# Splitting weights in one ScalarE pass, mixing in two matmul passes, and a later place for two steps of the next batch

## The chip, the cores and the metric

The kernel runs on one core of a Trainium2 chip. The metric is the device time of one execution in microseconds (us). A core has five engines that run their own instruction streams in order and wait for each other by semaphores: TensorE (PE: matmuls, and PEld, its weight loads), VectorE (DVE), ScalarE (ACT), GpSimd (POOL) and SyncE (SP), which here issues transfers between HBM and the on-chip memory SBUF. Matmuls write to PSUM banks. Times inside a run are us from the start of the span, the time from the first to the last instruction.

## The reference

Three blocks follow each other, for 8 batches of 576 rows (`S`), 8 heads of 64, 32 memory slots and a model width of 512:

```
a    = softmax(phi)                       # over the 576 rows
k_m, v_m = a^T k, a^T v                   # 32 slots per head
x    = softmax(q k_m^T / 8) v_m           # attention output, [576, 512]
h    = x^T U V                            # mixing over the rows, rank 32
u    = x + h^T
y    = u + relu(u w_ch1) w_ch2            # 512 -> 2048 -> 512
hh   = relu(y w_in);  u, v = halves of hh # 512 each
v_s  = w_spatial normalize(v) + b         # mixing over the rows
out  = (u * v_s) w_out
```

The matrices arrive in 32 bits (several of them as float64 values, which the kernel turns into 32-bit ones itself).

## The kernel before, in words

The work runs batch by batch, in half batches of 288 columns (`TH`), with five row tiles of 128 (`NST`; the fifth, the rest tile, has 64 rows). From batch 1 on, a factor is kept as two 16-bit halves, an upper and a lower one, and a product is three matmuls that add up in PSUM: upper by upper, upper by lower, lower by upper. Where the code says `for x, y in HI`, these are the three index pairs. An f32 matmul, used in batch 0, leaves two records in the profile.

Weights are loaded once. In batch 0 they are used in 32 bits while `conv_stream` converts them, and then `split_chunk` turns a chunk of 512 columns (288 for `w_spatial`) into the halves, in the place of the 32-bit chunk: ScalarE scales the chunk into a temporary tile (line 135), ScalarE copies it to the upper half (line 139), and VectorE subtracts to get the lower half (line 140). There are 54 chunks: `si` are those of `w_in` (8), `sw` of `w_spatial` (10), `s1` and `s2` of the two big matrices (16 each), `so` of `w_out` (4).

These splits, the norms of the spatial weights (`sn`), the conversion (`cs`) and the attention of batch 1 (`a1`) are generators. A `Filler` (lines 1020 to 1056) takes turns among those that are handed to it, a step at a time, as long as a budget lasts, and so mixes them into the matmul loops; `finish` runs one to its end. A scheduler then settles the order on each engine. Every engine's stream is fixed before the kernel runs.

The attention `att` of the next batch is spread in the same way over the loops of the present batch. Its parts here: the sums over rows of the softmax times U, the product `pps` (line 622, three matmuls per row tile, 96 columns of weights); `apr_sum` (lines 498 to 512), which adds the product with V and the attention weights themselves, transposed by a matmul with a scaled identity (line 509), in the three `at` banks; the largest value, spread over the partitions by a matmul with ones of a diagonal tile (`bmax_a` makes the diagonal, `bmax_b` issues the matmul, line 124); and the scaling into halves `apr` (lines 662 and 663), which empties the `at` banks. Behind it `z_gen` computes z, a product with w1 (line 693), again into `at` banks, 8 yields apart.

The stages of a batch are w1 (line 768; 722 in batch 0), w2 (line 805; 745 in batch 0), the scaling of y (`y_finish`), v and u (lines 876 and 945), spatial mixing with the gate (line 982), and the output (line 1005). In batch 0 the filler of the v and u stage has `a1, s1, so, s2`, and that of the spatial stage `a1, so, s1, s2`.

Of the kernel before, what the change touches and what calls it, by code (L numbers as in the profile page):

```python
# [30 lines left out]
def mixer_kernel(  # L31
# [52 lines left out]
    u3h = cp.tile([128, 2, NST, 96], F16, name="u3h")  # L84
    vst = cp.tile([96, S], F16, name="vst")
# [66 lines left out]
    def load_static():  # L152
        act.dma_start(ident, consts[:, 0:128])
        dve.memset(onesb, 1.0)
        pool.memset(ones32, 1.0)
        pool.memset(kmt, 0.0)

# [109 lines left out]
    def first(vr):  # L267
# [135 lines left out]
        ahl = tp.tile([128, NST, 2, 256], F16, tag="pa", name="ahl")  # L403

# [13 lines left out]
        def mix(ss):  # L418
            if not pps:
                pps.append(at_tile())  # L420
            for s in ss:
                r = rows(s)
                for i, (x, y) in enumerate(HI):
                    pe.matmul(pps[0][0:96, 0:256], u3h[:r, x, s, :], ahl[:r, s, y, :],
                              start=(s == 0 and i == 0), stop=(s == NST - 1 and i == 2))
# [19 lines left out]
        uh, ul = (u3h[:, i].rearrange("p s (e c) -> p s e c", c=M) for i in range(2))  # L445
        pool.tensor_copy(uh, ub)
        pool.tensor_tensor(out=ul, in0=ub, in1=uh, op=ALU.subtract)
# [5 lines left out]
        for h in range(2):  # L453
            act.activation(vst[:, h * TH:(h + 1) * TH], vr[1 + h][0], func=ACTF.Copy)
# [5 lines left out]
        for h in range(2):  # L460
            sl = slice(h * TH, (h + 1) * TH)
            pool.tensor_tensor(out=vst[32:64, sl], in0=vr[1 + h][0][32:64], in1=vst[32:64, sl], op=ALU.subtract)
        conv_b(*z0)
# [17 lines left out]
        pst = tp.tile([96, 256], F16, tag="pst", name="pst")  # L481
        act.activation(pst, pps[0][0:96, 0:256], func=ACTF.Copy, scale=2.0 ** -22)
# [15 lines left out]
    def apr_sum(pst, ahl, parts):  # L498
        ps = at_tile()
        o = 0  # L500
        for g, sa, sb in parts:
            n = min(sb * 128, S) - sa * 128
            pe.matmul(ps[:, o:o + n], pst[0:96, g * 128:(g + 1) * 128], vst[0:96, sa * 128:sa * 128 + n],
                      start=True, stop=False)
            for s in range(sa, sb):
                r = rows(s)
                for l in range(2):
                    oo = o + (s - sa) * 128
                    pe.matmul(ps[:, oo:oo + r], ahl[:r, s, l, g * 128:(g + 1) * 128], ident16[:r, :r],
# [4 lines left out]
    def att(b):  # L514
# [67 lines left out]
        ahl = tp.tile([128, NST, 2, 256], F16, tag="pa", name="ahl")  # L582
        for grp in ((0, 1), (2, 3), (4,)):
# [35 lines left out]
        for s in range(NST):  # L619
            r = rows(s)  # L620
# [802 lines left out]
```

## Time and profile before

| | us |
|---|---|
| median of 3 runs | 1189.0 (1183.98, 1189.0, 1189.25) |
| profiled execution | 1188.7 |
| its span | 1186.8 |
| TensorE busy in it | 1156.0 |
| VectorE busy | 690.3 |
| ScalarE busy | 533.5 |
| GpSimd busy | 65.4 |
| mean granted TensorE clock | 0.993 of 2.4 GHz |

Busy times are unions of an engine's instructions, so overlaps count once. A matmul's duration of 287 ns is the time through the array; the next one starts earlier, so that the pace of a stream is read from the start of one group to the start of the next. A bracket behind a row of the order of time is the idle time of that engine just before, with the instruction that ended it.

### The profile page before, as it was taken

What the parts mean: (1) busy time and instruction counts of PE and PEld (TensorE: products, weight loads), DVE (VectorE), ACT (ScalarE), POOL (GpSimd) and SP (SyncE); (2) the same over time, 40 slices, a digit from 0 to 9 for tenths busy, and PEclk for the clock granted to TensorE, in tenths of its full rate; (3) what the DMA queues carried; (4) which work ended last, traced back from release to release, by engine and by line L of the source; (5) the groups of instructions that cost most, each with busy time, mean ns of one, the idle gap of its engine ahead of it and who ended that gap; (6) DMA issues with size and microseconds to landing.
All of it is one profiled execution on the core that took longest, in us unless ns stands there. A gap on an engine that the chain in (4) does not pass through costs nothing.

```text
span 1186.8 us, 24260 instructions
## 1 busy us (share of the span) xinstructions
PE 1156.0 (97%) x10036; PEld 860.9 (73%) x10039; DVE 690.3 (58%) x1893; ACT 533.5 (45%) x1219; POOL 65.4 (6%) x251
## 2 busy tenths in 40 slices
PE   8898999899999999999999999999999999999998
PEld 6566767577677776777767776777767787677767
DVE  5766578657475474635665464754646465652454
ACT  4768885556245143442434242451434433442333
POOL 2001010000000000000000000100000000000000
PEclk9999999899999999999999999999999999999999
DMA  9776200140001400032001300014000200010001
GB/s 345 318 262 216 77 21 2 61 124 19 21 1 44 139 21 1 22 101 61 22 1 41 119 24 21 1 41 141 22 1 16 71 23 1 1 41 1 2 1 40
DMA packets 43005, 73.80 MB, mean 62 GB/s; under 512 B 6608, under 2 KB 34000, under 8 KB 39824
## 3 DMA queue, kind: packets, MB, share of 16 engines
q1 hardware_dynamic: 42384, 71.59, 17.8%
q8 instruction: 78, 1.28, 0.5%
q10 hardware_dynamic: 512, 0.67, 0.2%
q14 instruction: 31, 0.25, 0.1%
HBM read 62.82 MB, written 9.44 MB: 61 GB/s over the span
## 4 chain that ended last, share of the span: by engine, by line
PE 83%; DVE 6%; ACT 4%; DMA 4%; issue 1%; POOL 1%; POOLq 0%; ACTq 0%
PE mm L805 25%; PE mm L768 14%; PE mm L1005 8%; PE mm L945 7%; PE mm L982 7%; PE mm L876 6%; PE mm L745 4%; DMA kvt<-in_kv_dram 3%; PE at L590 2%; PE at L693 1%; PE at L540 1%; DMA qt<-in_qT_dram 1%; PE at L622 1%; PE mm L722 1%; PE mm L873 1%
## 5 line engine op out<-in xcount | busy, mean ns | idle before, releaser
L805 PE MATMUL mm<-g,w2r 128*128 128x288 f16 x2688 | 349.1, 287 | 0.0
L805 PEld LDWEIGHTS <-w2r 128*128 128x128 f16 x2688 | 257.6, 98 | 76.9 <-issue 14.2
L768 PE MATMUL mm<-apr,z 128*128 128x288 f16 x1344 | 167.5, 286 | 0.0
L768 PEld LDWEIGHTS <-z 128*128 128x128 f16 x1344 | 131.2, 98 | 32.9
L823 ACT ACTIVATE y<-mm 128x288 f32<-128x288 f32 x56 | 22.7, 406 | 208.0 <-DVE tiny L130 208.0
L777 DVE TENSOR_TENSOR g<-tmp,g 128x288 f16<-128x288 f32 x224 | 99.2, 456 | 20.1 <-ACT g L774 16.9
L982 PE MATMUL mm<-wsr,vu 128*128 128x288 f16 x768 | 104.7, 286 | 0.0
L772 ACT ACTIVATE tmp<-mm 128x288 f32<-128x288 f32 x224 | 91.7, 421 | 28.7 <-PE mm L768 14.5
L130 DVE TENSOR_REDUCE tiny<-mm 128x1 f32<-128x288 f32 x64 | 28.8, 453 | 124.1 <-PE mm L805 123.4
L1005 PE MATMUL mm<-ghl,wor 128*128 128x288 f16 x768 | 98.8, 290 | 0.0
L945 PE MATMUL mm<-yhl,wir 128*128 128x288 f16 x768 | 96.8, 286 | 0.0
L1005 PEld LDWEIGHTS <-wor 128*128 128x128 f16 x768 | 75.7, 99 | 26.4 <-issue 6.0
L945 PEld LDWEIGHTS <-wir 128*128 128x128 f16 x768 | 74.5, 98 | 21.6 <-issue 1.6
L982 PEld LDWEIGHTS <-vu 128*128 128x128 f16 x768 | 74.5, 98 | 18.7 <-DVE vu L928 0.3
L876 PE MATMUL mm<-wir,yhl 128*128 128x512 f16 x384 | 86.3, 379 | 0.0
L992 ACT ACTIVATE ghl<-vu,ysc 128x288 f16<-128x288 f32 x64 | 34.2, 534 | 83.3 <-DVE vu L991 61.6
L876 PEld LDWEIGHTS <-yhl 128*128 128x128 f16 x384 | 37.1, 98 | 41.4 <-issue 0.2
L745 PE MATMUL mm<-g,w2r 128*128 128x288 f32 x256 | 65.6, 408 | 0.1
L745 PEld LDWEIGHTS mm<-g,w2r 128*128 128x128 f32 x256 | 47.7, 190 | 15.2 <-issue 2.5
L776 DVE CAST g<-tmp 128x288 f16<-128x288 f32 x112 | 34.3, 306 | 41.0 <-ACT tmp L772 40.4
L1009 ACT ACTIVATE tmp<-mm,ysc 128x288 f32<-128x288 f32 x64 | 31.7, 497 | 38.6 <-PE mm L1005 37.6
L774 ACT ACTIVATE g<-mm 128x288 f16<-128x288 f32 x112 | 46.7, 417 | 0.0
(276 smaller groups left out, 1476.5 us busy)
## 6 DMA issues: line engine op xcount, KB each, us to landing
kvt<-in_kv_dram SPq DMA_DIRECT2D x28, 516.0 KB, 4.4
out_dram<-tmp SPq DMA_DIRECT2D x64, 144.0 KB, 1.7
qt<-in_qT_dram SPq DMA_DIRECT2D x28, 256.0 KB, 3.3
wir<-in_w_dram SPq DMA_DIRECT2D x6, 1024.0 KB, 7.7
e<-in_phi_dram SPq DMA_DIRECT2D x8, 512.0 KB, 4.1
phiT<-in_phiT_dram SPq DMA_DIRECT2D x7, 576.0 KB, 3.6
wor<-in_w_dram SPq DMA_DIRECT2D x3, 1024.0 KB, 7.0
wsr<-in_w_dram SPq DMA_DIRECT2D x3, 1024.0 KB, 6.8
```

Of the source, the lines that this page charges most:

```text
L745: pe.matmul(ps, w2r[:, f, d * 128:(d + 1) * 128], AT[0]["g"][:, f, :], start=False, stop=(f == 15))
L768: pe.matmul(ps, a["z"][:, k, x, f * 128:(f + 1) * 128], a["apr"][:, k, y, sl], start=(i == 0), stop=(i == 5))
L772: act.activation(r, ps, func=ACTF.Relu, scale=CG)
L774: act.activation(g[:, f, 0, :], ps, func=ACTF.Relu, scale=CG)
L776: dve.tensor_copy(g[:, f, 0, :], r)
L777: dve.tensor_tensor(out=g[:, f, 1, :], in0=r, in1=g[:, f, 0, :], op=ALU.subtract)
L805: pe.matmul(pss[d], w2h[:, f, x, d * 128:(d + 1) * 128], g[:, f, y, :], start=False, stop=(f == 15 and i == 2))
L876: pe.matmul(ps, yhl[:, k, x, s * 128:(s + 1) * 128], wih[:, k, 1, y, :], start=(i == 0), stop=(i == 11))
L945: pe.matmul(ps, wih[:, k, 0, x, d * 128:(d + 1) * 128], a["yhl"][:, k, y, sl], start=(i == 0), stop=(i == 11))
L982: pe.matmul(ps, vn[:, s, x, ds], wsh[:, s, th, y, :], start=(i == 0), stop=False)
L992: act.activation(ghl[:, d, 0, sl], u2, func=ACTF.Identity, scale=sgt)
L1005: pe.matmul(ps, woh[:, k, x, d * 128:(d + 1) * 128], a["ghl"][:, k, y, sl], start=(i == 0), stop=(i == 11))
```

## The change

- The halves of a weight change places: the lower comes first in memory. A chunk is now split by one ScalarE pass, which writes the scaled chunk in 16 bits to a temporary tile; VectorE computes the lower half from the 32-bit chunk in its place (a scalar_tensor_tensor), and then copies the upper half behind it. Every matmul that reads these weights takes the other index.
- The mixing product takes two matmuls per row tile. The weights have 128 columns: three copies of U's upper half, and its lower half; the second matmul has the three copies and a block of zeros. V gets a fourth block of 32 rows. The rest tile's lower 64 rows of `ahl` are set to zero by GpSimd, and all its matmuls have 128 rows.
- `third`, the filler of the second w1 half of batch 0, gets the splits of `w_in` from its fifth call on and the norms from its ninth, where it had the splits from the first and the norms from the fourth.
- The filler of the v and u stage of batch 0 has `a1, so`; `so` is finished before the spatial stage, whose filler has `a1, s1, s2`.
- `att_z` yields four times instead of twice before `z_gen`.

```diff
-    def split_chunk(raw, hi, lo, s, on_dve):
-        n = raw.shape[-1]
-        r = tmp()[:raw.shape[0], :n]
+    def split_chunk(raw, lo, hi, s):
+        r = tmp().bitcast(F16)[:, 0:raw.shape[-1]]
         act.activation(r, raw, func=ACTF.Identity, scale=s)
-        if on_dve:
-            dve.tensor_copy(hi, r)
-        else:
-            act.activation(hi, r, func=ACTF.Copy)
-        dve.tensor_tensor(out=lo, in0=r, in1=hi, op=ALU.subtract)
+        dve.scalar_tensor_tensor(out=lo, in0=raw, scalar=s, in1=r, op0=ALU.mult, op1=ALU.subtract)
+        dve.tensor_copy(hi, r)
...
         ahl = tp.tile([128, NST, 2, 256], F16, tag="pa", name="ahl")
+        pool.memset(ahl[64:128, 4], 0.0)
...
         for s in range(NST):
-            r = rows(s)
-            for i, (x, y) in enumerate(HI):
-                pe.matmul(pps[0:96, 0:256], u3h[:r, x, s, :], ahl[:r, s, y, :],
-                          start=(s == 0 and i == 0), stop=(s == NST - 1 and i == 2))
+            for y in range(2):
+                pe.matmul(pps[:, 0:256], u3h[:, y, s, :], ahl[:, s, y, :],
+                          start=(s == 0 and y == 0), stop=(s == NST - 1 and y == 1))
...
-        yield
-        yield
+        for _ in range(4):
+            yield
         yield from z_gen(b)
...
-            fl(1.5, cs, a1, si, *(() if nf[0] < 4 else (sn,)))
+            fl(1.5, cs, a1, *(() if nf[0] < 5 else (si,)), *(() if nf[0] < 9 else (sn,)))
...
-        vfill = (lambda dt: fl(dt, a1, s1, so, s2)) if b == 0 else (lambda dt: None)
+        vfill = (lambda dt: fl(dt, a1, so)) if b == 0 else (lambda dt: None)
...
         if b == 0:
-            vfill = lambda dt: fl(dt, a1, so, s1, s2)
+            fl.finish(so)
+            vfill = lambda dt: fl(dt, a1, s1, s2)
```

The rows of the order carry the line numbers of each kernel's own text. The split's lines are 135, 139 and 140 before, and 134 (ScalarE), 135 (scalar_tensor_tensor) and 136 (copy) after; line 622 is 621 after; the other lines named here agree.

TensorE, from the last apr sums of batch 1 (weights `ahl`, line 509) to the first output matmul of batch 0 (`wor`), with the spread matmul (`dgb`, line 124) between them, before:

```order
L509 MATMUL at<-ident_67,ahl 128x128
L509 LDWEIGHTS ahl
L509 MATMUL at<-ident_67,ahl 128x64
L509 LDWEIGHTS ahl
L509 MATMUL at<-ident_67,ahl 128x64
L124 LDWEIGHTS onesb
L124 MATMUL mm<-dgb,onesb 128x128
L1005 LDWEIGHTS wor
L1005 MATMUL mm<-ghl,wor 128x288
```

The same place after, where the last spatial matmuls (`wsr`) stand directly ahead of the spread matmul:

```order
L984 MATMUL mm<-wsr,vu 128x288
L985 LDWEIGHTS vu
L985 MATMUL mm<-wsr,vu 128x288
L124 LDWEIGHTS onesb
L124 MATMUL mm<-dgb,onesb 128x128
L1005 LDWEIGHTS wor
L1005 MATMUL mm<-ghl,wor 128x288
```

The apr sums are the same instructions and have moved ahead: after, the first of them stand behind the second v tile of batch 0 (line 876), the others behind the third and behind the second pair of u matmuls:

```order
L876 LDWEIGHTS yhl
L876 MATMUL mm<-wir,yhl 128x512
L503 LDWEIGHTS pst
L503 MATMUL at<-vst,pst 128x384
L509 LDWEIGHTS ahl
L509 MATMUL at<-ident_67,ahl 128x128
```

ScalarE, around the copies of y (line 754) at the end of the first w2 half of batch 0, with first and second passes of the splits of `w_in` (`wir`) and two exponentials of batch 1 (line 530), before:

```order
L135 ACTIVATE tmp<-wir,st 128x512 x2
L139 ACTIVATE wir<-tmp 128x512 x2
L135 ACTIVATE tmp<-wir,st 128x512
L754 ACTIVATE y_879<-mm 128x288 x4
L724 ACTIVATE g_900<-mm 128x288
L139 ACTIVATE wir<-tmp 128x512
L135 ACTIVATE tmp<-wir,st 128x512 x2
L139 ACTIVATE wir<-tmp 128x512 x2
L530 ACTIVATE e<-e 128x1024
L531 ACTIVATE e<-e 64x256
L139 ACTIVATE wir<-tmp 128x512
L724 ACTIVATE g_900<-mm 128x288
```

The same place after, where six splits stand ahead of the copies and the squares of the spatial weights (line 1179) come behind the exponentials:

```order
L134 ACTIVATE tmp<-wir,st 128x512 x6
L754 ACTIVATE y_878<-mm 128x288 x4
L724 ACTIVATE g_899<-mm 128x288 x2
L530 ACTIVATE e<-e 128x1024
L531 ACTIVATE e<-e 64x256
L724 ACTIVATE g_899<-mm 128x288 x2
L134 ACTIVATE tmp<-wir,st 128x512 x2
L1179 ACTIVATE tmp,amw<-wsr 128x288
L724 ACTIVATE g_899<-mm 128x288
L1179 ACTIVATE tmp,amw<-wsr 128x288 x2
```

Where before a split put two instructions on ScalarE, now it puts one, and the second of its two on VectorE's stream is the copy of line 136.

## Rows read from the trace of the kernel before

**Rows 1.** The page's busy times: engine, busy us, share of the span, instructions.

```profile
PE 1156.0 (97%) x10036; PEld 860.9 (73%) x10039; DVE 690.3 (58%) x1893; ACT 533.5 (45%) x1219; POOL 65.4 (6%) x251
```

**Rows 2.** Busy by stage: length, PE, PEld, DVE, ACT, POOL, granted clock, DMA, GB/s.

```profile
100.00:127.75 27.75, 23.85 (x160) 15.77 (x158) 14.69 (x42) 23.41 (x65) 1.43 (x7) 0.94 0.37 128
127.75:166.00 38.25, 38.25 (x201) 30.17 (x201) 25.23 (x62) 33.95 (x71) 2.95 (x6) 1.00 0.18 47
166.00:190.60 24.60, 24.60 (x175) 15.41 (x172) 19.77 (x75) 16.80 (x38) 1.36 (x7) 1.00 0.01 2
...
206.90:219.50 12.60, 7.86 (x50) 5.58 (x49) 8.65 (x23) 5.51 (x11) 1.37 (x6) 0.73 0.20 71
```

**Rows 3.** Order of time, TensorE, batch 2's mixing: start, length, engine, line, operation.

```profile
412.92 1.15 PE L622 MATMUL at<-ahl,u3h 128*96 128x256 f16 x9
413.90 0.90 PE L805 MATMUL mm<-g,w2r 128*128 128x288 f16 x6
414.64 0.95 PE L622 MATMUL at<-ahl,u3h 128*96 128x256 f16 x6
415.52 0.91 PE L805 MATMUL mm<-g,w2r 128*128 128x288 f16 x6
```

**Rows 4.** Groups by line and shape, weight loads: busy us, mean ns, idle.

```profile
L805 PEld LDWEIGHTS <-w2r 128*128 128x128 f16 x2688 | 257.6, 98 | 76.9 <-issue 14.2
...
L622 PEld LDWEIGHTS <-u3h 128*96 128x96 f16 x84 | 9.6, 123 | 0.7
```

**Rows 5.** Order of time, TensorE, a stream of 128-wide weights at the start.

```profile
22.38 5.42 PE L150 MATMUL mm<-ones,onesb 128*128 128x256 bf16 x48
```

**Rows 6.** Order of time, TensorE, the two z chunks (line 693) of batch 2.

```profile
436.78 3.10 PE L805 MATMUL mm<-g,w2r 128*128 128x288 f16 x24
...
442.31 6.05 PE L805 MATMUL mm<-g,w2r 128*128 128x288 f16 x48
448.30 1.03 PE L693 MATMUL at<-w1r,vmt 64*32 64x512 f16 x25
...
449.72 2.50 PE L805 MATMUL mm<-g,w2r 128*128 128x288 f16 x19
```

**Rows 7.** Waits of TensorE, 300 to 1190 us: total us, count, mean.

```profile
PE at L693 <- DVE apr L663: 2.6, 5, 0.6
```

**Rows 8.** Order of time, TensorE, behind the spatial stage of batch 0.

```profile
211.67 0.26 PE L124 MATMUL mm<-dgb,onesb 128*128 128x128 bf16 x1 [4.74 <-DVE dgb L118]
...
211.73 8.07 PE L1005 MATMUL mm<-ghl,wor 128*128 128x288 f16 x48
```

**Rows 9.** Order of time, 100 to 110 us, around the keys' load (`kvt`).

```profile
101.43 3.07 PE L722 MATMUL mm<-apr,z 128*128 128x288 f32 x12
...
104.98 1.09 PE L540 MATMUL at<-kvt,e 128*32 128x129 f32 x32 [0.48 <-ACT e L530]
...
105.69 4.57 SPq L243 DMA_DIRECT2D kvt<-in_kv_dram  x3
...
109.05 0.65 PE L540 MATMUL at<-kvt,e 128*32 128x129 f32 x16 [2.98 <-DMA kvt<-in_kv_dram]
```

**Rows 10.** Groups by line and shape, the splits and like operations.

```profile
L776 DVE CAST g<-tmp 128x288 f16<-128x288 f32 x112 | 34.3, 306 | 41.0 <-ACT tmp L772 40.4
...
L928 DVE SCALAR_TENSOR_TENSOR vu<-tmp,mv,vu 128x512 f16<-128x512 f32 x32 | 22.7, 747 | 9.6 <-ACT vu L927 9.6
...
L118 DVE TENSOR_SCALAR dgb<-identb,tiny 128x128 bf16<-128x128 bf16 x52 | 13.2, 254 | 1.7
...
L140 DVE TENSOR_TENSOR w1r<-tmp,w1r 128x512 f16<-128x512 f32 x16 | 10.8, 687 | 6.9 <-ACT w1r L139 6.8
...
L139 ACT ACTIVATE w1r<-tmp 128x512 f16<-128x512 f32 x16 | 9.7, 619 | 0.0
```

**Rows 11.** Order of time, VectorE and TensorE, batch 1's last half of `ahl`.

```profile
272.72 0.69 DVE L612 TENSOR_TENSOR ahl<-tmp,ahl 128x512 f16<-128x512 f32 x1 [0.37 <-ACT ahl L611]
...
273.48 0.93 PE L622 MATMUL at<-ahl,u3h 128*96 128x256 f16 x7
```

More of the change, by code (lines that the diff above doesn't have):

```diff
@@ L83, in mixer_kernel @@
     wsr = cp.tile([128, NST, 2, TH], F32, name="wsr")
[L84 to L85 removed]
+    u3h = cp.tile([128, 2, NST, 128], F16, name="u3h")
+    vst = cp.tile([128, S], F16, name="vst")
     bb = cp.tile([128, S], F32, name="bb")
@@ L156, in load_static @@
         pool.memset(kmt, 0.0)
+        pool.memset(u3h[:, 1], 0.0)
     def conv_load(src, raw, eng=sp):
@@ L444, in first @@
         ub = ur.rearrange("p (s c) -> p s c", s=NST).unsqueeze(2).to_broadcast([128, NST, 3, M])
-        uh, ul = (u3h[:, i].rearrange("p s (e c) -> p s e c", c=M) for i in range(2))
+        uh, ug = (u3h[:, i, :, 0:96].rearrange("p s (e c) -> p s e c", c=M) for i in range(2))
         pool.tensor_copy(uh, ub)
-        pool.tensor_tensor(out=ul, in0=ub, in1=uh, op=ALU.subtract)
+        pool.tensor_tensor(out=u3h[:, 0, :, 96:128], in0=ur.rearrange("p (s c) -> p s c", s=NST),
+                           in1=u3h[:, 0, :, 0:32], op=ALU.subtract)
+        act.activation(ug, ub, func=ACTF.Copy)
         conv_low(z0[1], dve)
@@ L480, in first @@
         mix((4,))
-        pst = tp.tile([96, 256], F16, tag="pst", name="pst")
-        act.activation(pst, pps[0][0:96, 0:256], func=ACTF.Copy, scale=2.0 ** -22)
+        pst = tp.tile([128, 256], F16, tag="pst", name="pst")
+        act.activation(pst, pps[0][:, 0:256], func=ACTF.Copy, scale=2.0 ** -22)
         dve.scalar_tensor_tensor(out=pst[64:96], in0=pps[0][64:96, 0:256], scalar=2.0 ** -22, in1=pst[64:96],
@@ L508, in apr_sum @@
                     oo = o + (s - sa) * 128
-                    pe.matmul(ps[:, oo:oo + r], ahl[:r, s, l, g * 128:(g + 1) * 128], ident16[:r, :r],
+                    pe.matmul(ps[:, oo:oo + r], ahl[:, s, l, g * 128:(g + 1) * 128], ident16[:, :r],
                               start=False, stop=(s == sb - 1 and l == 1))
@@ L582, in att @@
         ahl = tp.tile([128, NST, 2, 256], F16, tag="pa", name="ahl")
+        pool.memset(ahl[64:128, 4], 0.0)
         for grp in ((0, 1), (2, 3), (4,)):
@@ L619, in att @@
         for s in range(NST):
-            r = rows(s)
-            for i, (x, y) in enumerate(HI):
-                pe.matmul(pps[0:96, 0:256], u3h[:r, x, s, :], ahl[:r, s, y, :],
-                          start=(s == 0 and i == 0), stop=(s == NST - 1 and i == 2))
+            for y in range(2):
+                pe.matmul(pps[:, 0:256], u3h[:, y, s, :], ahl[:, s, y, :],
+                          start=(s == 0 and y == 0), stop=(s == NST - 1 and y == 1))
             if s == 2:
                 yield
-        pst = tp.tile([96, 256], F16, tag="pst", name="pst")
-        act.activation(pst, pps[0:96, 0:256], func=ACTF.Copy, scale=2.0 ** -22)
+        pst = tp.tile([128, 256], F16, tag="pst", name="pst")
+        act.activation(pst, pps[:, 0:256], func=ACTF.Copy, scale=2.0 ** -22)
         dve.scalar_tensor_tensor(out=pst[64:96], in0=pps[64:96, 0:256], scalar=2.0 ** -22, in1=pst[64:96],
@@ L1004, in out_half @@
                 for x, y in HI:
-                    pe.matmul(ps, woh[:, k, x, d * 128:(d + 1) * 128], a["ghl"][:, k, y, sl],
+                    pe.matmul(ps, woh[:, k, 1 - x, d * 128:(d + 1) * 128], a["ghl"][:, k, y, sl],
                               start=(i == 0), stop=(i == 11))
```

37 lines of the change are left out of this document (19 added, 18 removed).

## The prediction, made before the changed kernel was run

> **What bounds the kernel now.** I read the page's busy shares first, then the busy time by stage, then who waits for whom, then the order of time at the places that the change touches. TensorE is busy for 97% of the span [rows 1], so what counts is what shortens its stream or closes one of its gaps: 1186.8 - 1156.0 = 30.8 us idle in all. The stages tell where [rows 2]: between 100 and 127.75 us TensorE is busy 23.85 of 27.75 us at a mean granted clock of 0.94, while ScalarE is busy 23.41; from 127.75 to 190.6 us it has no gap; between 206.9 and 219.5 us it is busy 7.86 of 12.6 us at a clock of 0.73. From batch 1 on the stream is nearly closed, and only short waits stand in it. So ScalarE bounds one stretch of batch 0, a chain on VectorE one point behind its spatial stage, and TensorE's own stream the rest.
>
> The sums are against the profiled execution: 1188.7 us, of which the span is 1186.8 and 1.9 lie around it. The median of the three runs, 1189.0, is the same within 0.3; they lie 5.3 apart, so the level is uncertain by 2 or 3 us whatever the change does.
>
> **Mixing in two passes.** Before, 15 matmuls a batch (three for each of five row tiles, line 622) take the PE from 412.92 to 413.90 and from 414.64 to 415.52, so 0.98 + 0.88 = 1.86 us [rows 3]. The first nine run at 0.109 each; the last six, three of them of 64 rows, at 0.147. After, it is 10 matmuls, all 128 rows by 128 columns. A stream of 128x256 passes with 128-wide weights takes 5.42 us for 48, so 0.113 each [rows 5], and ten take 1.13. That saves 0.73 a batch, and because TensorE has no slack there it is all on the path: 7 x 0.75 = 5.3 us, with 0.2 for batch 0, whose mixing waits for VectorE anyway. Bounds: 4.4 in all if ten loads at the old 123 ns set the pace, 6.2 if batch 0 saves five whole passes. The full-height rest tile in the second use (line 509) changes no count of instructions; loads of 64 and 128 rows run at one pace there, and I cost it at nothing.
>
> A 128x96 load takes 123 ns and a 128x128 load 98 [rows 4]: the wider is the faster. The Trainium skill, TensorE: Matmul & The Clock Gate, section LDWEIGHTS (loading the stationary operand), says that a load's time grows with its columns, whatever its rows, which speaks against padding 96 to 128; by it the old passes would have been bound by the stream alone, and dropping five of them would be worth 5 x 0.113 x 7 = 4.0 us, not 5.3. The row decides against it here. (The same page's section on weight-path modes has a fast load for exactly 128 weights of a 16-bit type, and that is what the row looks like.)
>
> The zero fill of the rest tile is one 64x512 memset a batch on GpSimd, which is idle 94% of the time. For batch 2 it waits for the reading of phiT on VectorE, and the scale of the first gating stage is queued behind it on GpSimd; the gate results are needed only 14 us later, so it costs nothing unless phiT lands very late.
>
> **The later z product.** Two more yields put the first z chunk 12 matmuls later. Before, its first matmul waits for the banks that line 663 empties: the 24 matmuls from 436.78 on end near 439.7, and the next of line 805 starts at 442.31, so the chunk holds the PE for 2.6 us, while the second z chunk, which waits for nothing, starts at 448.30, behind 48 matmuls that end near 448.2, and gives way at 449.72, 1.5 us [rows 6]. Twelve matmuls at 6.05 / 48 = 0.126 are 1.5 us, more than the 1.1 lost. Batches 1 to 6 each have this once: 6 x 1.0 = 6.0 us; bounds 2.6 (five waits that carry the label [rows 7]) and 6.4. What is late next is the second chunk, which moves by the same 12 matmuls and keeps its distance.
>
> **Attention of batch 1 out of the spatial stage.** In batch 0 the last pieces of batch 1's attention stand behind the spatial stage, and their scale needs a VectorE chain queued behind the gating and two output-weight splits. TensorE idles 4.74 us before the matmul of line 124, and the 48 matmuls behind it take 8.07 us [rows 8], in a stretch whose granted clock averages 0.73 [rows 2], partly at 1.2 GHz, where 48 of the same shape take 6.05 at 2.4 GHz [rows 6]. The change takes s1 and s2 out of the filler of the u/v stage, so that attention gets every second turn; the order shows the apr sums among the v matmuls and only the single spread matmul behind the spatial stage, its diagonal long ready. Gain 4.74 + 2.02 = 6.8 us. The 7 + 7 + 10 apr matmuls are the same ones. What hides the work that moves in: VectorE was busy 19.77 of 24.6 us in 166 to 190.6 [rows 2]; four output splits and three reductions replace five splits there, about 2.4 us more by the durations below, which leaves some 2 us of cover, and the TensorE work that moves in adds 1 to 2 us more. Bounds: 3 if a new wait of that size stands before the spatial stage, 7.3 at best.
>
> **The stretch 100 to 127.75 us.** ScalarE paces it. Each split costs it two passes now and one after; by the order, six second passes of w_in (0.62 each [rows 10]), one of w1 and one of the spatial weights leave this stretch, about 4.8 us, and the squares of the spatial weights come later. The keys of row tile 2 are loaded when tile 0 has been read: the load is issued at 105.69 and the matmul gets it at 109.05 after 2.98 us of idling. In the new order six matmuls of line 722 (two records and 0.51 us each [rows 9]) and a spread stand between: 3.1 us, which covers it. Against that, six splits now stand ahead of the copies that free the banks of the first half (line 754), some 1.5 us later. Gain: 2.98 for the load, 1 for ScalarE and the clock, 4.0 in all; bounds 0 and 5.6, the latter all 3.9 us of idling and the 0.06 x 27.75 = 1.7 us that the clock withheld.
>
> **The splits on VectorE.** 54 chunks. ScalarE loses a second pass of 0.62 on 44 and a shorter one on 10: about 31 us of work, off the path nearly everywhere. VectorE's subtraction of 687 ns becomes a scalar_tensor_tensor like line 928's, 747 ns, and a copy from 16 to 16 bits that the trace of before does not have [rows 10]. Bounds for the copy: 0.25, a 128-wide 16-bit operation, and 0.687, full rate. I take 0.306, the cast of 288 words in line 776, because 512 halves are 256 words. So a chunk costs VectorE 1.05 where it cost 0.69; with 0.3 on the narrow ones, 44 x 0.366 + 10 x 0.3 = 19 us more. In 127.75 to 166 about 24 chunks fall: 25.2 + 8.3 = 33.5 busy of 38.25 us, so TensorE still sets the pace. If that cover is gone, each further us is on the path.
>
> Batch 1 is where it shows. One w2 chunk is split ahead instead of three, so 15 stand in its w2 stage: 15 x 1.05 - 13 x 0.69 = 6.8 us more on VectorE. Before, the last low half of ahl for tiles 2 and 3 ends at 273.41 and the matmuls on it start at 273.48 [rows 11]: no slack. The rest tile's ahl and chunk 14 then come about 1 us late. I take 1.2 us lost; bounds 0 and 3.
>
> **Sum.** 5.5 + 6.0 + 6.8 + 4.0 - 1.2 = 21.1 us. 1188.7 - 21.1 = 1167.6 us.
>
> **Rivals.** (a) *VectorE takes the gain of batch 0.* The stretch to 127.75 gains nothing and the heavier VectorE adds 3 us of waits in batches 0 and 1: 1188.7 - (5.5 + 6.0 + 6.8) + 3 = 1173.4, up to 1178 if the attention moved into the u/v stage waits too. For it: ScalarE work that goes to an engine busy 88% of a stretch. Against it: TensorE has a closed stream there, with work ahead of each wait. (b) *The waits only move.* The banks are freed by the same chain, and z waits again; behind the spatial stage the ghl chain is late instead. Then the mixing and the stretch to 127.75 remain: 1188.7 - 5.5 - 4.0 + 1.2 = 1180.4. Against it: twelve matmuls exceed the measured gap, and batches 1 to 7 pass from the spatial stage to the output without a gap. (c) *Slower: the copy costs full rate.* At 0.687 a split costs VectorE 1.43: 24 x 0.38 = 9 us more in 127.75 to 166, 42.6 us of work in 38.25; the decision point is a copy of about (38.25 - 33.5) / 24 + 0.31 = 0.5 us. If in-order VectorE then delays every piece that TensorE waits for, all 19 + 44 x 0.38 = 36 us less the idle VectorE time of these stages (about 13 + 5) are on the path, +18, and the attention again spills behind the spatial stage: 1188.7 + 18 - 5.5 - 6.0 = 1195. Against it: the two-source operations run at 1.3 ns a column, the single-source cast at 1.06 with its fixed part in it. (d) *The split change does nothing:* no separate case, since ScalarE is not TensorE's bound outside the one stretch.
>
> **How the numbers follow.** Forecast 0.65, its own range 1162 to 1173 (its bounds, narrowed because they will not all fall on one side). (a) 0.20, (b) 0.10, (c) 0.05. All terms at their low bounds give 1188.7 - (4.4 + 2.6 + 3 + 0 - 3) = 1181.7, all at the high ones 1163.2, and the level wanders by 2 or 3 us. The range is 1160 to 1180, which leaves out (c) and part of (b). What a measurement can tell from no change is about 0.5%, 5.9 us: faster means below 1183.1. That holds for the forecast, for (a) and for most of (b): 0.90. Within: 0.05, the rest of (b) and a mild (c). Slower: 0.05.
>
> **What would show it.** Ten records a batch of line 621, loads near 98 ns, some 1.1 us; no idle time on the first z chunk, 1.5 us from line 805 to line 805; no 4.7 us gap behind the spatial stage, and the output matmuls there 48 in 6 us; the w2 stage of batch 0 beginning near 124 instead of 127.75. The copy (line 136) near 0.3 us. Wrong would be TensorE waits with VectorE's splits as releaser between 125 and 190 or 243 and 280 us, a wait on line 518 before the spatial stage, or a copy of 0.5 us and more.

## The result and the profile after

The changed kernel took 1158.09 us (median of 4 runs, 1157.63 to 1159.77) beside 1186.73 for the kernel before on the same chip: a ratio of 0.9762, 95% interval 0.9731 to 0.9792, faster. On a second chip it was 1156.23 beside 1182.99, a ratio of 0.9783 (0.9766 to 0.9799). The direction was right; the time lies 1.9 us below the range of 1160 to 1180, and 9.5 below the 1167.6 of the sum.

The profiled execution took 1157.6 us, its span 1155.8. The page's busy times of the changed kernel, which answer to [rows 1]:

```profile
PE 1137.3 (98%) x9999; PEld 850.9 (74%) x9999; DVE 699.5 (61%) x1947; ACT 508.5 (44%) x1166; POOL 71.9 (6%) x261
```

TensorE lost 18.7 us of work and 12.3 of its 30.8 us of idle time. VectorE gained 9.2 us, where the prediction had 19, and ScalarE lost 25. The stages of batch 0, after (columns as in [rows 2]; up to 121.20 the end of w1, then w2, u/v, spatial mixing, output):

```profile
98.30:121.20 22.90, 22.84 (x180) 15.55 (x178) 17.66 (x57) 21.23 (x60) 3.32 (x10) 1.00 0.55 188
121.20:158.26 37.06, 37.06 (x188) 29.22 (x181) 30.89 (x89) 23.28 (x45) 1.32 (x6) 1.00 0.13 37
158.26:183.47 25.21, 25.21 (x194) 16.67 (x193) 19.72 (x79) 12.71 (x28) 1.36 (x7) 1.00 0.08 25
183.47:197.36 13.89, 13.89 (x117) 11.12 (x115) 11.61 (x32) 5.36 (x15) 2.53 (x9) 1.00 0.01 2
197.36:216.34 18.98, 16.19 (x197) 10.76 (x196) 13.08 (x28) 12.35 (x25) 1.48 (x6) 1.00 0.14 48
```

The 3.9 us of idling ahead of the second w2 half are gone, and the clock there is 1.00 instead of 0.94. VectorE has 30.89 of 37.06 us in the stage that the prediction feared, and TensorE none idle. The spatial stage is closed, and behind it, where [rows 8] had a wait of 4.74 us, no bracket stands:

```profile
197.31 0.22 PE L124 MATMUL mm<-dgb,onesb 128*128 128x128 bf16 x1
197.36 6.04 PE L1005 MATMUL mm<-ghl,wor 128*128 128x288 f16 x48
```

The mixing of batch 2, after, answers to [rows 3]:

```profile
394.84 0.82 PE L622 MATMUL at<-ahl,u3h 128*128 128x256 f16 x6
395.49 0.90 PE L805 MATMUL mm<-g,w2r 128*128 128x288 f16 x6
396.23 0.60 PE L622 MATMUL at<-ahl,u3h 128*128 128x256 f16 x4
396.66 0.90 PE L805 MATMUL mm<-g,w2r 128*128 128x288 f16 x6
```

From 394.84 to 395.49 and from 396.23 to 396.66 it is 0.65 + 0.43 = 1.08 us, where it was 1.86. (The trace has it at line 622, as before.) The z chunks of batch 2, against [rows 6]:

```profile
421.93 1.03 PE L693 MATMUL at<-w1r,vmt 64*32 64x512 f16 x25
...
423.35 6.05 PE L805 MATMUL mm<-g,w2r 128*128 128x288 f16 x48
429.33 1.03 PE L693 MATMUL at<-w1r,vmt 64*32 64x512 f16 x25
```

No bracket stands behind the first chunk, and it gives way to line 805 after 1.42 us, as the second does. The splits, against [rows 10]:

```profile
L135 DVE SCALAR_TENSOR_TENSOR w1r<-w1r,st,tmp 128x512 f16<-128x512 f32 x16 | 11.6, 742 | 0.0
...
L134 ACT ACTIVATE tmp<-w1r,st 128x512 f16<-128x512 f32 x16 | 10.9, 708 | 0.0
...
L136 DVE COPY w1r<-tmp 128x512 f16<-128x512 f16 x16 | 4.2, 280 | 0.0
```

The copy that no row of before showed takes 280 ns, close to the 306 taken and far from the full rate of 687. But these durations can't be added up: in the order of time of VectorE the next instruction starts before the one ahead of it has ended.

```profile
231.03 0.49 DVE L136 COPY w2r<-tmp 128x512 f16<-128x512 f16 x2
231.44 1.41 DVE L135 SCALAR_TENSOR_TENSOR w2r<-w2r,st,tmp 128x512 f16<-128x512 f32 x2
232.76 0.49 DVE L136 COPY w2r<-tmp 128x512 f16<-128x512 f16 x2
```

From start to start two copies take 0.41 us and two operations of line 135 take 1.32, so in such a row a chunk occupies VectorE for 0.20 + 0.66 = 0.86 us and not for the 1.05 of the prediction.

Stage lengths say more than the totals: TensorE's stream is in the same order in each execution of a kernel, and the stages without transfers or waits agree within 0.03 us. They are taken from the first matmul of one stage to that of the next; "again" are second traces (below).

| us | before (1188.7) | before again (1182.8) | after (1157.6) | after again (1155.6) |
|---|---|---|---|---|
| up to the first w1 matmul | 39.96 | 37.77 | 37.94 | 37.51 |
| w1 and w2 of batch 0 | 126.13 | 125.69 | 120.32 | 120.27 |
| u/v, batch 0 | 24.51 | 24.51 | 25.21 | 25.21 |
| spatial, batch 0 | 21.13 | 21.12 | 13.89 | 13.89 |
| output, batch 0 | 19.08 | 18.85 | 18.98 | 18.97 |
| first w2 half to the end of the second, batch 1 | 77.40 | 77.61 | 74.21 | 73.63 |
| the same, batches 2 to 6 | 381.55 | 378.37 | 367.75 | 366.79 |

All other stages are the same within 0.1 us in the four traces, but for the last one, the output of batch 7 to the end of the span: 15.3 us in both traces of before and 15.7 in both of after. Its matmuls take 11.92 us in all four; the 0.4 us come behind the last of them, and no run shows why.

### The profile page after: what moved, and what is told of

Its sections match the earlier page's. It is cut to its first block, busy times and chain, and to the rows that moved or that the text cites. A ratio compares the mean times of both kernels' runs of the same rounds, so it can differ in the third digit from the quotient of the medians.

```text
span 1155.8 us, 24236 instructions
## 1 busy us (share of the span) xinstructions
PE 1137.3 (98%) x9999; PEld 850.9 (74%) x9999; DVE 699.5 (61%) x1947; ACT 508.5 (44%) x1166; POOL 71.9 (6%) x261
## 4 chain that ended last, share of the span: by engine, by line
PE 86%; DVE 6%; ACT 3%; DMA 3%; issue 1%; POOL 0%; ACTq 0%; DVEq 0%; POOLq 0%
PE mm L805 26%; PE mm L768 14%; PE mm L1005 8%; PE mm L945 7%; PE mm L982 7%; PE mm L876 6%; PE mm L745 4%; PE at L591 2%; DMA kvt<-in_kv_dram 2%; PE at L540 1%; PE at L693 1%; PE mm L722 1%; PE mm L873 1%; PE mm L798 1%; PE at L722 1%; PE mm L984 1%
```

## The experiments

Each run is compared with the kernel before on its own chip; as the levels of chips and executions wander by some us, the verdict on an edit rests on the stage lengths against the second trace of the changed kernel. The columns are the stages of the table above, the first of them from the first w2 matmul of batch 0 on. The opening 40 us are left out; they differ by -0.3 to +3.7 us, and why isn't known.

| us more than "after again" | w2, b. 0 | u/v | spatial | output | w2, b. 1 | b. 2 to 6 |
|---|---|---|---|---|---|---|
| apr sums: 64-row rest tile | +1.08 | +0.42 | 0 | -0.42 | +0.93 | +2.17 |
| two yields | +0.01 | 0 | 0 | 0 | +1.03 | +6.57 |
| u/v fillers as before | +0.02 | -0.50 | +6.63 | -0.38 | +0.18 | +1.10 |
| w1 filler as before | +0.97 | 0 | 0 | -0.10 | +0.52 | +0.76 |
| split as before | +2.33 | 0 | 0 | -0.71 | +0.75 | +0.99 |
| both | +5.91 | +0.39 | 0 | -0.80 | +0.19 | +0.77 |
| copy twice | -0.31 | +1.11 | 0 | +0.03 | +0.88 | +0.30 |
| mixing as before | +0.48 | +0.02 | 0 | +0.28 | +1.14 | +2.97 |
| mixing as before, 128 rows | -0.11 | +0.02 | 0 | +0.29 | +0.60 | +3.11 |
| keys later | -0.49 | -0.53 | +4.84 | -0.29 | +1.02 | +1.97 |
| six yields | +0.01 | +0.01 | -0.01 | +0.01 | +0.31 | -0.22 |
| only a1 in u/v | +0.03 | +0.78 | +4.50 | -1.92 | +0.25 | +1.90 |
| a1 in u/v, so in spatial | +0.01 | +0.78 | +1.13 | +2.81 | +0.39 | +0.85 |

The first trace of the changed kernel differs from the second by +0.58 and +0.96 in the last two columns: that much is chance of the transfers.

**The changed kernel again**, no edit.

> The changed kernel itself, unaltered, as the level for the runs beside it. Both accounts: 1158 us (1157.6 to 1159.8 so far). Its new trace shows which waits for DMA recur: if the 1.7 us that TensorE waits for the keys of row tiles (line 540) in the first trace are chance, they stand at other batches or sum to another figure; if the order of the work sets them, the same three batches show them again.

1156.23 us, span 1153.8. The waits for keys were 1.0 us in three places where they had been 1.7 in three; two of the three are the same places (in the stages of batches 3 and 6). Partly set by the order, partly chance.

**The kernel before again**, no edit.

> The kernel before, unaltered, for a second trace. Its first trace, on which the sum was made, is of an execution of 1188.7 us; seven runs beside the first experiments had a median of 1183.0. Theory: the difference is waits of TensorE for the transfers of keys and queries (7.3 us in the first trace) and what follows them (24 matmuls of line 805 in 4.7 us instead of 3.0 behind one of them); in an execution near 1183 they are under 4 us, and the stages without attention agree within 0.1 us. Rival: the level comes from the opening 40 us, or from a slower clock spread over the run.

1182.81 us, span 1181.0, so 5.9 below the execution on which the sum was made. Of the difference 2.2 lie in the opening 40 us, where both accounts had a part, and 2.9 in batch 3. There the first trace has (order of time, TensorE)

```profile
541.46 1.97 PE L590 MATMUL at<-kmt,qt 128*128 128x64 f32 x16 [1.24 <-DMA qt<-in_qT_dram]
543.27 4.77 PE L805 MATMUL mm<-g,w2r 128*128 128x288 f16 x24
```

and the second, at the same place,

```profile
537.22 2.03 PE L590 MATMUL at<-kmt,qt 128*128 128x64 f32 x16
539.08 3.10 PE L805 MATMUL mm<-g,w2r 128*128 128x288 f16 x24
```

One late load of queries cost 1.24 us of waiting and 1.7 us more, since the granted clock of 543.27 to 547.90 was 0.63. All waits of TensorE for keys and queries came to 5.7 us beside 7.3 in the first trace, more than the 4 expected. The wait of 2.98 us for the keys in batch 0 [rows 9] came again (2.94), as did two in batch 1 (0.76 and 0.99 in the first trace, 1.03 and 0.88 in the second): those belong to the order of the kernel before.

**The rest tile in the apr sums.**

```diff
-  pe.matmul(ps[:, oo:oo + r], ahl[:, s, l, ...], ident16[:, :r], ...)
+  pe.matmul(ps[:, oo:oo + r], ahl[:r, s, l, ...], ident16[:r, :r], ...)
```

> The changed kernel with one thing undone: in the apr sums (line 509) the rest tile's matmuls with the scaled identity have 64 rows again, not 128 padded ones; the mixing keeps its padded rest tile. Theory from the two traces: four such matmuls a batch take 0.37 us with 64 rows and 0.17 with 128, twice a batch, so 0.40 a batch and 3.2 over eight: 1161.3 us. Rival, the step of the prediction that costed this edit at nothing: 64 and 128 rows run at one pace, 1158.1 us, and the 0.40 seen in the traces came from the neighbouring edit (128 rows of pst).

1161.47 us, ratio 0.9826 (0.9809 to 0.9842). In batch 2, with 64 rows (order of time, TensorE; lines 503 and 509 alternate with nothing between):

```profile
415.75 0.44 PE L509 MATMUL at<-ident,ahl 128*128 128x128 f16 x4
416.12 0.26 PE L503 MATMUL at<-vst,pst 128*128 128x192 f16 x1
416.21 0.44 PE L509 MATMUL at<-ident,ahl 128*128 128x128 f16 x4
```

and in the changed kernel with 128:

```profile
414.74 0.33 PE L509 MATMUL at<-ident,ahl 128*128 128x128 f16 x4
414.91 0.25 PE L503 MATMUL at<-vst,pst 128*128 128x192 f16 x1
415.00 0.33 PE L509 MATMUL at<-ident,ahl 128*128 128x128 f16 x4
```

Four matmuls, the last two of each group on the rest tile, hold TensorE from 415.75 to 416.12, 0.37 us, against 0.17. So the padding is worth 0.20 a group and 0.40 a batch on line 509, in every batch, and the rival falls. Not all of it is time: in batch 0 the u/v stage is 0.42 longer and the output stage 0.42 shorter, since there TensorE waits for apr 0.81 us instead of 1.22. The medians show 5.2 rather than 3.2: another 1.0 us lies in batch 0's w2 stage, 0.7 of it a wait for `dgb`, in an order of instructions that is the same; this part isn't explained.

**The same edit alone, on the kernel before.**

```diff
+  pool.memset(ahl[64:128, 4], 0.0)
-  pe.matmul(ps[:, oo:oo + r], ahl[:r, s, l, ...], ident16[:r, :r], ...)
+  pe.matmul(ps[:, oo:oo + r], ahl[:, s, l, ...], ident16[:, :r], ...)
```

> The kernel before with one part of the change: the rest tile of ahl is zero in its lower 64 rows, and its matmuls with the scaled identity in the apr sums have 128 rows. Theory: 0.20 us less for each group of four matmuls, twice a batch, 0.40 a batch: 3.2 in eight batches, 1183.3 to 1180.1 us, and the stages show it batch by batch. Rival, the prediction's: nothing, 1183.3. In the changed kernel undoing it cost 5.2 by the medians and 4.1 by the profiles, so more than 3.2 is possible.

1184.62 beside 1186.49 us, ratio 0.9985 (0.9969 to 1.0002): -1.9 by the medians, with an interval that holds 1, so the total shows no difference. Line 509 takes 0.40 us less in each of batches 1 to 6, 2.39 in all, against the second trace of before; 0.75 of it went back in longer waits for keys (in batch 1 the wait was 1.50 us here). The term is real, its share of the total is blurred by the transfers.

**Two yields ahead of z.**

```diff
-  for _ in range(4):
+  for _ in range(2):
       yield
   yield from z_gen(b)
```

> The changed kernel with two yields ahead of z instead of four. Theory: the first z chunk again stands 12 matmuls too early, waits 0.5 us for the bank and runs at a slower pace; 1.0 us in each of batches 1 to 5 and nothing in batch 6, so +5.0: 1163.1 us. Rival: most of the gain in these stages came from transfers that landed sooner and from the narrower work ahead, not from z; then under +2: below 1160 us.

1164.80 us, ratio 0.9849 (0.9834 to 0.9864). The waits are back, in five batches (waits of TensorE):

```profile
PE at L693 <- DVE apr L663: 2.8, 5, 0.8
```

The six w2 stages are 7.6 us longer: 2.66 is time of line 693, which runs slower behind the wait (1.93 us for the first chunk of batch 2, beside 1.42), 2.86 is the waits, and 1.4 is longer waits for keys. So z's place is worth 1.0 us a batch in batches 1 to 5 and 0.5 in batch 6, 5.5 in all; the other 2.1 us are not z's.

**Six yields.**

```diff
-  for _ in range(4):
+  for _ in range(6):
```

> The changed kernel with six yields ahead of z instead of four. Theory (12 matmuls exceed the chain that empties the banks, so nothing is left to gain, and the second chunk still ends 8 yields ahead of the next stage or is drained there): same, 1156.5 us; the z chunks take 1.42 us each again. Rival: z ends up behind the w2 stage, and the w1 stage of the next batch waits for it: 1 us a batch, 1162 us.

1157.41 us, ratio 0.9782 (0.9759 to 0.9805): the same as the changed kernel. Twelve matmuls exceed the chain, and twelve more gain nothing.

**The fillers of the u/v and spatial stage as before.**

```diff
-  vfill = (lambda dt: fl(dt, a1, so)) if b == 0 ...
+  vfill = (lambda dt: fl(dt, a1, s1, so, s2)) if b == 0 ...
-  fl.finish(so)
-  vfill = lambda dt: fl(dt, a1, s1, s2)
+  vfill = lambda dt: fl(dt, a1, so, s1, s2)
```

> The changed kernel with the filler lists of the u/v and spatial stage of batch 0 as before (a1, s1, so, s2 and a1, so, s1, s2, without finishing so). Theory: the last apr sums go behind the spatial stage again and the 4.7 us gap with its slow output matmuls comes back, net of what it cost elsewhere (the first trace: +0.7 in the u/v stage, -7.2 in the spatial stage, 0.1 behind it): +6.6, 1164.7 us. Rival: the order of the lists mattered little, and the lighter ScalarE work of the new split closed most of that gap: under +3, below 1161 us.

1164.93 us, ratio 0.9852 (0.9837 to 0.9866). The wait for `dgb` behind the spatial stage is back:

```profile
204.52 0.26 PE L124 MATMUL mm<-dgb,onesb 128*128 128x128 bf16 x1 [5.52 <-DVE dgb L118]
```

The spatial stage is 6.63 us longer; u/v and output give back 0.9. Net 5.75, and the new split does not close that gap by itself.

**The w1 filler as before, the split as before, and both.**

```diff
   (w1 filler)
-  fl(1.5, cs, a1, *(() if nf[0] < 5 else (si,)), *(() if nf[0] < 9 else (sn,)))
+  fl(1.5, cs, a1, si, *(() if nf[0] < 4 else (sn,)))
   (split)
-  r = tmp().bitcast(F16)[:, 0:raw.shape[-1]]
+  r = tmp()[:, 0:raw.shape[-1]]
   act.activation(r, raw, func=ACTF.Identity, scale=s)
-  dve.scalar_tensor_tensor(out=lo, in0=raw, scalar=s, in1=r, ...)
-  dve.tensor_copy(hi, r)
+  act.activation(hi, r, func=ACTF.Copy)
+  dve.tensor_tensor(out=lo, in0=r, in1=hi, op=ALU.subtract)
```

> The changed kernel with the filler of the second w1 half of batch 0 as before: the splits of w_in from the first call, the norms from the fourth. Theory (the later start of the splits is what lets the keys' load and the copies of the first half come in time): the 3.0 us wait for the keys of row tile 2 comes back and the w2 stage of batch 0 is some 3 us longer, +3 on 1156.5, 1159.5 us. Rival (the single ScalarE pass alone cleared that stretch): within 1 us of the changed kernel, 1156.5 us. Batch by batch nothing else should move.

> The changed kernel with a chunk split as before (ScalarE scales to 32 bits and copies to the upper half, VectorE subtracts), all lists and yields as changed. Theory (the split itself bought the part of the 5.9 us that the list does not explain): +3 in the w2 stage of batch 0, 1159.5 us, and batch 1 about as it is, since its VectorE was not late. Rival, the prediction's account of the splits: VectorE's lighter work gives 1.2 us back in batch 1 while ScalarE takes 4 in batch 0, 1159.3 in all, but the stages differ: batch 1's w2 stage 1.2 us shorter than 73.6.

> The changed kernel with both undone that bear on the first w2 half of batch 0: the split as before and the filler of the second w1 half as before. Alone, the list gave 1.0 and the split 2.3 us in the w2 stage of batch 0. Theory (the prediction's: ScalarE paces that stretch, and the two help each other): together they give back all of the 5.9 us, the wait of 3.0 us for the keys of row tile 2 included: 1162.5 us. Rival (they add up, and the rest was the late transfer of one execution): 3.3 us, 1159.8.

1158.06 us (ratio 0.9778, 0.9758 to 0.9798), 1159.13 (0.9793, 0.9764 to 0.9823) and 1164.96 (0.9822, 0.9797 to 0.9846). Alone the two cost 1.0 and 2.3 us in batch 0's w2 stage, together 5.9: either is enough to let the keys land in time, and only without both does the wait return. With both undone:

```profile
105.04 1.09 PE L540 MATMUL at<-kvt,e 128*32 128x129 f32 x32
109.42 1.09 PE L540 MATMUL at<-kvt,e 128*32 128x129 f32 x16 [3.29 <-DMA kvt<-in_kv_dram]
```

In the changed kernel line 722 and the spread stand between, as the prediction had it, with no bracket:

```profile
103.59 1.09 PE L540 MATMUL at<-kvt,e 128*32 128x129 f32 x32
104.62 1.24 PE L722 MATMUL mm<-apr,z 128*128 128x288 f32 x4
105.69 0.22 PE L124 MATMUL mm<-dgb,onesb 128*128 128x128 bf16 x1
105.75 2.16 PE L722 MATMUL mm<-apr,z 128*128 128x288 f32 x8
107.84 0.65 PE L540 MATMUL at<-kvt,e 128*32 128x129 f32 x16
```

The wait is followed by a lower clock (busy by stage, columns as in [rows 2]; first with both undone, then the changed kernel):

```profile
109.42:114.40 4.98, 4.93 (x33) 3.16 (x36) 1.38 (x2) 4.25 (x17) 0.00 (x0) 0.68 0.25 88
109.00:114.00 5.00, 5.00 (x39) 3.35 (x38) 3.15 (x8) 4.94 (x19) 0.00 (x0) 1.00 0.53 159
```

So of the 5.9 us, 3.3 are the wait and 0.32 x 4.98 = 1.6 the clock behind it; the other 1.0 are not told apart. With the split alone undone, batch 1 did not become shorter but 0.75 longer, 0.76 of it a wait for queries: no burden of VectorE shows there.

**The copy made twice.**

```diff
   dve.tensor_copy(hi, r)
+  dve.tensor_copy(hi, r)
```

> The changed kernel with VectorE's copy of the upper half made twice: 44 x 0.28 + 10 x 0.22 = 14.5 us more on VectorE, nothing else. Theory (VectorE is covered by TensorE's stream wherever splits run): less than 1 us, below 1157.5. Rival, the prediction's terms for VectorE (each us that is added behind the ahl halves of batch 1 is late, and 24 chunks fall in batch 0's second w2 half): 15 x 0.28 = 4 us in batch 1 and up to 3 in batch 0, 1160 to 1163 us.

1159.27 us, ratio 0.9794 (0.9768 to 0.9820). Its busy times:

```profile
PE 1135.5 (98%) x9999; PEld 850.1 (74%) x9999; DVE 708.9 (61%) x2001; ACT 508.8 (44%) x1166; POOL 73.8 (6%) x261
```

VectorE is busy 9.4 us longer than in the changed kernel, not 14.5: 54 copies at 0.17 each, by the start-to-start times. The stages of batches 0 and 1 are 1.7 us longer in all, more than the theory's 1 and far less than the rival's 4 to 7; but the order of the stages changed a little too (two mixing passes, 0.2 us, moved into the u/v stage), and the two traces of the changed kernel lie 0.6 apart in batch 1. What names VectorE as the releaser is 0.54 us of waits in the u/v stage and 0.60 in batch 1, beside none and 0.15 in the changed kernel: some of VectorE's work is uncovered, about a tenth of what was added.

**The mixing as before, with the rest tile at 64 rows and at 128.**

```diff
-  for y in range(2):
-      pe.matmul(pps[:, 0:256], u3h[:, y, s, :], ahl[:, s, y, :], ...)
+  for i, (x, y) in enumerate(HI):          # u3h 96 columns wide again
+      pe.matmul(pps[0:96, 0:256], u3h[:r, x, s, :], ahl[:r, s, y, :], ...)
   (second kernel: [:, x, s, :] and [:, s, y, :], all 128 rows)
```

> The changed kernel with the mixing product as before: three passes, 96 columns of weights, the rest tile's passes with 64 rows; the apr sums keep their padded rest tile. Theory and the prediction's first term agree: 0.77 us a batch in seven batches and 0.2 to 0.5 in batch 0, +5.7: 1162.2 us. Rival (the passes were hidden behind the waits for ahl and z, which take their place): under +3, since in batches 1 to 6 the later z chunk would be reached later and its wait shrink.

> The changed kernel with the mixing in three passes of 96 columns as before, but all 15 passes of a batch with 128 rows (the rest tile padded). With the rest tile's passes at 64 rows the mixing took 1.86 us a batch, in two passes 1.08. Theory (each change of row height costs TensorE about 0.2 us, as in the apr sums): 0.37 less than 1.86, so 1.48 a batch; of the 0.78 gained, half is the padding and half the five passes. Rival, the prediction's account (passes at 0.11 to 0.12 each and no price for 64 rows): 15 x 0.109 = 1.64 or more, up to 15 x 0.123 = 1.85 by the loads of 96 columns. Total against the changed kernel +2.8 (theory) or +4 to +5.7: 1159.3 or 1160.5 to 1162.2.

1162.31 us (ratio 0.9816, 0.9795 to 0.9836) and 1160.97 (0.9806, 0.9788 to 0.9824). With 64 rows the mixing takes 1.86 us a batch again in batches 2 to 6. With 128 (its lines are two lower):

```profile
395.36 1.15 PE L620 MATMUL at<-ahl,u3h 128*96 128x256 f16 x9
396.35 0.90 PE L803 MATMUL mm<-g,w2r 128*128 128x288 f16 x6
397.08 0.82 PE L620 MATMUL at<-ahl,u3h 128*96 128x256 f16 x6
397.74 0.90 PE L803 MATMUL mm<-g,w2r 128*128 128x288 f16 x6
```

0.99 + 0.66 = 1.65 us for 15, so 0.11 each, and 0.11 is also what the ten passes with 128 columns take. Of the 0.78 that the change gained a batch, 0.21 is the rest tile's height and 0.57 the five passes. The stage lengths of the two kernels don't show the 0.21: in batches 2 to 6 TensorE waited 1.1 us for keys and queries with 128 rows and 0.4 with 64. The expectation of 1.48 was wrong: three passes at 64 rows cost 0.21 more together, not 0.37. In the mixing and in the apr sums alike, going to 64 rows and back costs about 0.2 us once, for three passes as for two.

It is not the change of height as such. In the kernel before, line 503 goes from 128 rows to 96 between two groups of line 509 (order of time, TensorE):

```profile
39.04 0.25 PE L503 MATMUL at<-vst,pst 96*128 96x192 f16 x1
39.13 0.44 PE L509 MATMUL at<-ident,ahl 128*128 128x128 f16 x4
```

From 39.04 to 39.13 it is 0.09 us; in the changed kernel the same matmul with 128 rows takes 0.08 (414.66 to 414.74 in its trace). Why 64 rows cost something and 96 don't stays open.

**The keys one yield later.**

```diff
   for s in grp:
       yield
       yield
+  yield
```

> The changed kernel with one more yield behind each group of key tiles in the attention, so that the loads of the next tiles have one more turn of TensorE's work to land in; all later steps come up to three turns later. Theory: the 1.0 to 2.4 us that TensorE waits for keys in the traces go, and nothing else waits: 1155.3 against 1156.5 us. Rival: the later z comes too close to the end of the w2 stage, or the apr sums of batch 1 fall behind again: 2 us or more slower, over 1158.5.

1163.21 us, ratio 0.9804 (0.9780 to 0.9829), by its stages slower than the changed kernel. Three more turns put the spread behind the spatial stage again (+4.84, with 3.7 us of waiting for `dgb`), and the keys still had 1.9 us of waits.

**Only a1 in the u/v filler, and so in the spatial stage.**

```diff
-  vfill = (lambda dt: fl(dt, a1, so)) if b == 0 ...
+  vfill = (lambda dt: fl(dt, a1)) if b == 0 ...
   (second kernel, also)
-  fl.finish(so)
-  vfill = lambda dt: fl(dt, a1, s1, s2)
+  vfill = lambda dt: fl(dt, a1, so, s1, s2)
```

> The changed kernel with only a1 in the filler of the u/v stage of batch 0 (so is then split in one go ahead of the spatial stage). By the order, the apr sums stand 24 to 48 matmuls earlier and the spread matmul in the u stage, no longer behind the spatial stage. Theory (the 1.2 us wait for apr and 1.3 for z in batch 0's output stage come from the place of the spread): 2 us faster than the changed kernel, 1154.5. Rival: four splits of w_out in one go delay the gate's VectorE work, and TensorE waits 1 to 3 us at the spatial stage instead: 1157 to 1159 us.

> As the run with only a1 in the filler of the u/v stage, but the splits of w_out are mixed into the spatial stage (filler a1, so, s1, s2) instead of made in one go ahead of it. By the order, z's first matmul then stands ahead of the third group of 24 output matmuls. Theory: 2 us faster than the changed kernel, 1154.5, and no wait at the spatial stage. Rival: the output matmuls wait for the halves of w_out, or z for its chain as before: 1156.5 us or more.

1161.96 us (ratio 0.9812, 0.9790 to 0.9833) and 1161.93 (0.9818, 0.9794 to 0.9843). The theory held for its own place: in the first kernel the output stage is 1.92 us shorter. But the spatial stage pays 4.5, of which 2.3 are waits and, behind them, the granted clock was 0.52 over 2.7 us:

```profile
185.23 0.90 PE L982 MATMUL mm<-wsr,vu 128*128 128x288 f16 x6
187.74 0.42 PE L982 MATMUL mm<-wsr,vu 128*128 128x288 f16 x2 [1.62 <-ACT vu L927]
188.53 0.96 PE L982 MATMUL mm<-wsr,vu 128*128 128x288 f16 x4 [0.37 <-DVE vu L928]
```

In the second the halves of w_out come late to the output:

```profile
209.25 5.94 PE L1005 MATMUL mm<-ghl,wor 128*128 128x288 f16 x24 [2.08 <-DVE wor L136]
215.12 1.54 PE L693 MATMUL mm<-w1r,vmt 64*32 64x512 f16 x47
```

The wait is 2.08 us, and the 24 matmuls behind it take 5.87 instead of 3. No run beat the changed kernel beyond what the measurement can tell.

## Why the prediction was off

**What held.** From the second trace of before to the second of after, 1181.0 - 1153.8 = 27.2 us of span went, where the sum had 21.1. By term:

| us | forecast | measured |
|---|---|---|
| mixing in two passes | 5.5 | 5.4 |
| later z | 6.0 | 5.2 |
| attention out of the spatial stage | 6.8 | 5.8 |
| the stretch up to the second w2 half | 4.0 | 5.2 |
| splits on VectorE, batch 1 | -1.2 | -0.1 |
| full-height rest tile in the apr sums | 0 | 2.4 |
| waits for keys and queries in batch 1 | not in the sum | 1.9 |
| not told apart | | 1.4 |

The last row is made of tenths: in batches 1 to 6 the scores (line 590 before, 591 after) and lines 805 and 798 take some 0.3 us a batch less, by what isn't known, and the end of the span takes 0.4 more.

- The mixing: 0.77 a batch in batches 1 to 6 and 0.8 in batch 0, against 0.75 forecast. The size was right, as the difference of two rows of the trace; the reason was half wrong: the forecast took it all for five passes, and the runs give 0.57 to the passes and 0.21 to the row height. On the weight load the prediction set the row [rows 4] against the Trainium skill (TensorE: Matmul & The Clock Gate, LDWEIGHTS (loading the stationary operand)): the 96-wide loads do take 123 ns and the 128-wide 98, in the last runs too, but passes with either run at 0.11 us, so the load's length does not matter here. The 4.0 us that followed if the stream alone counts is what the passes gave: 0.57 x 7 = 4.0.
- The attention out of the spatial stage: -7.23 there, +0.70 and +0.12 beside it, and of these 6.4 us 0.6 are three mixing passes that stood in the u/v stage before. The two us of slow output matmuls came back as forecast (48 in 6.04 us), but 1.23 of waiting for apr and 0.4 more for z stand in the output stage now, which the prediction did not have.
- The stretch up to the second w2 half: 5.4, of which 0.2 is mixing, within its bounds (0 to 5.6). It came by the step named, the keys' load covered by line 722. The term was under-sized: it had 2.98 for the load and 1 for ScalarE and the clock together, and the clock alone withheld 1.6 behind that wait.
- The later z: 2.7 us of line 693 and waits of 0.5 in batches 1 to 5, so 5.2 of the 6.0 forecast. Undoing it in the changed kernel costs 5.5.

**The step that failed** is the sentence on the full-height rest tile in the second use: "loads of 64 and 128 rows run at one pace there, and I cost it at nothing". Loads do (94 and 98 ns in the trace of before); the stream does not. It is worth 0.40 a batch, 2.4 in batches 1 to 6; the 0.4 of batch 0's u/v stage go into a longer wait in the output stage. The row stood in the trace: in [rows 3] the last six mixing passes ran at 0.147 and the first nine at 0.109, and the prediction read that as a price of the mixing alone. It was carried to one of the two uses of the rest tile only.

**A loss that did not come**: "I take 1.2 us lost" for VectorE in batch 1. The prediction added up recorded durations, 19 us more on VectorE; the page has 9.2, in part because an operation starts before the one ahead has ended (0.86 us a chunk from start to start, 1.02 by durations). The rest tile's low half of `ahl` did come about one us later in the stage, but TensorE had other matmuls there, and one wait of 0.15 us stands in each trace of after with VectorE's split as releaser. The doubled copy shows how little VectorE weighs: 9.4 us of work, 1.0 us of new waits. [rows 11] showed "no slack" of a wait that the scheduler's new order moved; a zero distance in one order isn't a price in another.

**A term that was missing**: in batch 1 the waits for keys and queries (1.9 us in the second trace of before) are gone in both traces of after. With the old split 0.76 and 0.20 returned, with the old w1 filler 0.23 and 0.16, with both 0.21, so neither edit accounts for it, nor do the two together; what does is left open.

**The base.** The sum was made against an execution of 1188.7 us, 2.0 above the median of four on its own chip and 5.7 above that of seven on the second, since it held a late transfer with a slow clock behind it and a slow opening. The prediction said that the level wanders by 2 or 3 us. From 1186.73 the same sum gives 1165.6, so the base makes 2.0 of the 9.5 us; the other 7.5 are gain that the sum did not have, 28.6 us for 21.1. With every term at its best bound it came to 1163.2, still above the measured time: the range went down to 1160 for the wandering level, and no choice within the bounds of its terms would have reached the result.

The rivals fell: VectorE did not take batch 0's gain (a), the waits did not move back (b), but for 1.6 us in the output stage of batch 0, the copy did not run at full rate (c).

## What to carry to other kernels

Where a tile of 64 rows stands among f16 matmuls of 128, read from start to start what the visit costs, and look for it in every place that reads the tile: padding it with zeros can be the cheapest microsecond. Durations of neighbouring instructions on one engine may overlap; take what a stream costs from its starts. Before a sum is hung on one profiled execution, look for waits in it that a second execution would not have, and take the base from the runs, not from that trace. Two edits that clear the same wait can't be measured one at a time: undo both.

## What was not expected of the hardware

- In a row of f16 matmuls of 128 rows, a visit to weights of 64 rows costs about 0.2 us: 0.20 for two passes of line 509, 0.21 for three of line 622. A visit to 96 rows does not (0.09 us beside 0.08, line 503). In the f32 product of line 540 no such price shows either: in the changed kernel 16 matmuls of 64 rows hold TensorE for 0.57 us (115.57 to 116.14), 16 of 128 for 0.58.
- A wait can be paid twice. Granted clock by stretch (the last kernel above, the second with only a1 in the u/v filler, from 206.00 on: nearly idle, then the 24 output matmuls, then the work behind them; columns as in [rows 2]):

```profile
206.00:209.20 3.20, 0.37 (x1) 0.01 (x1) 3.17 (x9) 1.32 (x3) 0.00 (x0) 0.88 0.00 0
209.25:215.10 5.85, 5.85 (x24) 3.45 (x24) 1.60 (x3) 2.75 (x5) 0.00 (x0) 0.50 0.14 50
215.12:222.00 6.88, 6.88 (x126) 3.85 (x126) 3.77 (x6) 5.24 (x11) 0.00 (x0) 0.99 0.20 67
```

TensorE worked 0.37 of 3.2 us, and the clock behind was 0.50, the lower of its two levels (1.2 of 2.4 GHz): 2.9 us lost beside the wait. In the changed kernel's output stage, with waits of 1.2 and 1.3 us between stretches of matmuls, the clock stayed at 1.00. In the kernel before, the wait of 1.24 us in batch 3 was followed by a mean clock of 0.63 over 4.6 us, and with the old split and w1 filler that of 3.29 us by 0.68 over 5.0.
